# A recurrence and a gated layer in one kernel: three units of 512 tokens in the ramp, y in two tiles, and a new order list

## The chip, the cores and the metric

The kernel runs on one core of one Trainium2 chip. The metric is the device time of one execution in microseconds (us), median of three. The engines of the core are TensorE (PE, with its weight loads shown as PEld), VectorE (DVE), ScalarE (ACT), GpSimd (POOL) and SyncE (SP), whose queue issues nearly all DMAs. Each takes its instructions in its own order and waits for the others by semaphores.

## The reference

Two stages over 4 sequences of 6,336 tokens, 25,344 tokens of 256 features:

```python
sig = 1.0 / (1.0 + np.exp(-f_logit))
f = lower_bound + (1.0 - lower_bound) * sig
i = 1.0 - f
for t in range(S):
    h = f[:, t] * h + i[:, t] * x[:, t]
    y[:, t] = h
...
H = np.maximum(y @ w_h, 0.0)
T = 1.0 / (1.0 + np.exp(-(y @ w_t + b_t)))
out = T * H + (1.0 - T) * y
```

Input and output are float32. x and f_logit are read once and the output is written once, 25.95 MB each.

## The kernel before

The tokens are cut into 28 units, one after the other: 256, 256, 512, 23 of 1,024, 512 and 256 tokens (`parts`, L42, counts blocks of 128). A unit is loaded with tokens on the partitions, turned so that the 256 features lie in two halves on the partitions, scanned along the tokens, sent through the two matrix products and turned back. Nothing in the kernel picks the order: `order` (L48 to L98) is a list of tokens written out in full, and the loop at its end (L384 to L394) calls `do_<letter>` for each and pins each instruction in its engine's program order. A token such as `b2.1v:0` is step, unit, part or half, `v` for "on VectorE", and the buffer slot after the colon. [...]

The steps of a unit, with engine and line:

- `l`, `x`: loads of f_logit and x, issued by SyncE (L244)
- `u`: sigmoid(-f_logit), which is one minus the sigmoid, on ScalarE (L256)
- `b`: the product bv = u * x, on GpSimd, or on VectorE with `v` (L264)
- `i`: turns u to uT on TensorE, through PSUM (L271); `f`: f = 1 + ncc * uT on ScalarE or, with `v`, VectorE (L280, L282)
- `p`: turns bv to bT on TensorE (L291)
- `s`: the scan y = f * y + bT of one half on VectorE (L308), which reads f from SBUF and bT from PSUM; at the start of a sequence it is cut in two pieces
- `g`, `z`: the two matrix products, of both halves of y, on TensorE (L320, further columns with the same weights L114)
- `t`: the sigmoid of z on ScalarE (L333); `d`: max(g, ncc * y) on VectorE (L337), with y from SBUF and g from PSUM
- `e`: the product d * t, both from SBUF, on GpSimd or, with `v`, VectorE (L343), in the pieces that the fourth entry of a unit gives: 2,048 columns are a whole unit of 1,024 tokens
- `o`: turns y (times a diagonal of cc) and d back and adds them on TensorE (L365, L366); `c`: copies the sum from PSUM on ScalarE or, with `v`, VectorE; `w`: the store, issued by SyncE (L382)

Once only: `pc`, `cc`, `dg` make constants of lower_bound, `pb` and `cb` of the bias, `wt` and `wh` load the weights, `WT` and `WH` scale them on VectorE. The scan's result is kept without the factor 1 - lower_bound = cc, which is put into the weights and the diagonal.

What sets the order around the change:

- Each engine runs its own steps in list order, and waits for the data and for the slot of its result. uT and bT take turns in two PSUM slots (a0, a1), all other PSUM results in three pairs of banks (b0 to b2), at the end the a slots too.
- SyncE's queue holds loads and stores in list order; a store waits there for its copy, and what stands behind it waits too.
- `shared` (L178) remembers the last product of VectorE in the list. The next GpSimd product in the list waits for it. A VectorE product never waits for a GpSimd one that stands ahead of it.

y is one tile of 2,048 columns for each unit, in four slots, the halves side by side (`flat`, `half`).

Of the kernel before, what the change touches and what calls it, by code (L numbers as in the profile page):

```python
# [53 lines left out]
e1.1 e1.0 k*2:0 w0.0 u4:1 z2.0:1 f3.0:1 z2.1:0 b4.0:1 s3.1:0 p3.0:0 o1.0:2 t2.1:0 u27:0 b4.1 c1.0:1 s3.0 w1.0 x8:3  # L54
i4.0:1 g2.0:0 f4.0:0 d2.0 i4.1:1 p4.0:0 l9:1 x9:4 l11:4 t2.0 u5:2 e2.1v e2.0v z3.0:0 g3.1:1 b27.0:0 z3.1:2 s4.0:1
p4.1:0 f4.1:1 i5.0:1 t3.0:0 t3.1 d3.1:1 b5.0:2 g3.0:0 f5.0:0 s4.1 o2.0:1 u6:1 b5.1 c2.0:2 d3.0 w2.0 i5.1:1 x11:0 e3.2
g4.1:2 p5.0:0 d4.1:0 b6.0:1 f5.1:1 s5.0:2 z4.1:0 t4.1:1 p5.1:1 b6.1 u7:2 e3.1 s5.1 l10:0 z4.0:1 t4.0 g4.0:0 i6.0:0
e3.0v p6.0:1 d4.0 o3.0:1 e4.2 b7.0:2 f6.0:0 s6.0:3 e4.0v i6.1:0 b7.1 u8:3 f6.1:1 o3.1:0 c3.0:0 c3.1:1 w3.1 w3.0 g5.0:2
p6.1:0 i8.1:1 z5.0:1 f8.1:0 x10:1 e4.1 t5.0:0 g5.1:0 i7.1:1 b8.0:1 s6.1 i7.0:0 d5.0:1 z5.1:1 l12:2 f7.1:1 p7.1:1 d5.1
f7.0:2 t5.1 b8.1 g6.0:2 p7.0:0 e5.1 k*3:0 o4.1:1 s7.1:0 z6.0:0 d6.0:2 s7.0 u9:1 b9.0:2 g6.1:2 c4.1:3 d6.1 i9.0:1  # L60
t6.0:1 b9.1 o4.0:1 u11:2 i9.1:0 f9.0v:1 c4.0:2 w4.0 e6.0v f9.1:2 g7.1:0 z6.1:2 k*3:1 e5.2v i8.0:1 z7.0:1 e5.0v t6.1
w4.1 f8.0:3 p8.1:0 d7.1:0 t7.0:0 g7.0:2 e6.1 p8.0:1 b11.0:3 o5.0:0 u10:1 c5.0:0 w5.0 x12:2 o5.1:1 c5.1:1 w5.1 s8.1:1
i11.1:0 z7.1:0 f11.1:0 s8.0 b11.1 l13:0 d7.0 p9.0:1 i10.1:0 z8.0:1 e6.2 b10.1:1 g8.1:2 t7.1 f10.1:3 p9.1:0 s9.0:2
# [5 lines left out]
z11.0:2 i13.0:1 p12.0:0 s12.0 o9.0:0 t11.0 f13.0:2 g11.0:1 d11.0 o9.1:2 e11.0 p13.0:1 c9.0:1 u17:1 i14.0:0 f14.0v:1
c9.1:3 g12.0:0 u15:3 d12.0:2 b15.1:2 w9.0 z12.1:1 i17.0:0 f17.0:3 t12.1:1 o10.0:2 s13.0:2 o10.1:0 p13.1:0 c10.0:0  # L70
s13.1 b15.0 c10.1:1 i14.1:1 g12.1:1 z12.0:2 g13.0:0 i15.0:0 l16:1 f14.1:2 d12.1 p14.0:1 x16:2 d13.0:0 t12.0 o11.0:1
w9.1 g13.1:2 s14.0:3 f15.0:0 p14.1:0 o11.1:0 e12.0 w10.0 w10.1 i15.1:1 c11.0:2 u16:2 x17:1 b16.1:1 b16.0 z13.0:1 d13.1
f15.1:1 c11.1:0 z13.1:2 s14.1 t13.1:0 l18:0 t13.0 w11.0 p15.0:1 o12.1:0 i16.0:0 g14.1:2 s15.0:0 d14.1:1 e13.0 o12.0:1
p15.1:1 s15.1 c12.1:1 b17.1:2 f16.0:2 z14.1:0 z14.0:2 p16.0:0 s16.0:1 c12.0:3 t14.1:1 t14.0 g14.0:1 d14.0 i16.1:1
w11.1 l19:1 u18:3 x18:0 b17.0 e14.0 g15.1:0 d15.1:2 z15.0:2 i17.1:0 x19:3 f16.1:0 b18.0:3 p16.1:1 f17.1:1 b18.1 l20:2
s16.1 o13.1:1 t15.0:0 p17.0:0 g15.0:0 w12.1 d15.0 c13.1:0 u19:1 b19.1:1 o13.0:2 p17.1:1 z15.1:1 c13.0:2 z16.0:0
s17.1:2 t15.1 t16.0:1 z16.1:2 s17.0 g16.0:1 w13.1 t16.1 i18.0:1 d16.0:0 g16.1:0 o14.0:2 i18.1:0 f18.0:0 d16.1 e15.0v
# [223 lines left out]
    def half(n, key, h):  # L301
        return st[n][key][:, h * tokens(n):(h + 1) * tokens(n)]

    def do_s(n, h, eng, slot):
        flat(n, "y", "y", slot)
        y = half(n, "y", h)
        for fresh, c, e in pieces(n):
            pin(nc.vector.tensor_tensor_scan(y[:, c:e], st[n]["f", h][:, c:e], st[n]["bT", h][:, c:e],  # L308
# [114 lines left out]
```

## Time and profile before

| | before |
|---|---|
| median of three executions | 207.93 us (207.89 to 208.76) |
| span of the profiled execution, first to last instruction | 206.1 us |
| busy: PE, DVE, ACT, POOL | 192.6, 194.5, 191.9, 173.8 us |
| bytes moved by DMA | 78.7 MB, 382 GB/s over the span |

One execution was profiled; its span is 206.1 us, and no other time of that execution is given. A row of a list by time gives the start and the length in us, engine, line, operation, output and inputs with their shapes, how many like it follow, and in brackets how long the engine sat idle before it and what ended that. A row of a group gives the shape, the count, the busy time, the mean length of one in ns, and the idle time before. A row of a stretch gives the busy time of PE, PEld, DVE, ACT and POOL in it, the granted TensorE clock, the share of the DMA engines and GB/s.

### The profile page before, as it was taken

What the parts mean: (1) busy time and instruction counts of PE and PEld (TensorE: products, weight loads), DVE (VectorE), ACT (ScalarE), POOL (GpSimd) and SP (SyncE); (2) the same over time, 40 slices, a digit from 0 to 9 for tenths busy, and PEclk for the clock granted to TensorE, in tenths of its full rate; (3) what the DMA queues carried; (4) which work ended last, traced back from release to release, by engine and by line L of the source; (5) the groups of instructions that cost most, each with busy time, mean ns of one, the idle gap of its engine ahead of it and who ended that gap; (6) DMA issues with size and microseconds to landing.
All of it is one profiled execution on the core that took longest, in us unless ns stands there. A gap on an engine that the chain in (4) does not pass through costs nothing.

```text
span 206.1 us, 4635 instructions
## 1 busy us (share of the span) xinstructions
PE 192.6 (93%) x1837; PEld 133.8 (65%) x1837; DVE 194.5 (94%) x159; ACT 191.9 (93%) x192; POOL 173.8 (84%) x93
## 2 busy tenths in 40 slices
...
DVE  0899999999999999999899999999999999999972
...
POOL 3036989789979997999999999799899999998840
...
GB/s 196 370 424 422 411 418 423 409 423 417 414 423 408 429 417 426 423 420 413 425 424 416 433 411 417 429 415 418 407 422 422 414 392 378 286 104 204 138 382 248
DMA packets 16125, 78.68 MB, mean 382 GB/s; under 512 B 1764, under 2 KB 2536, under 8 KB 10216
## 3 DMA queue, kind: packets, MB, share of 16 engines
...
q10 hardware_dynamic: 8, 0.00, 0.0%
HBM read 52.43 MB, written 25.95 MB: 380 GB/s over the span
## 4 chain that ended last, share of the span: by engine, by line
PE 53%; ACT 14%; DMA 13%; DVE 10%; issue 6%; POOL 2%; SPq 1%; ACTq 0%; DVEq 0%; POOLq 0%
DMA x<-in_x_dram 9%; DVE y L308 8%; PE op L366 7%; PE bT L291 7%; PE op L365 7%; PE g L320 7%; PE z L320 6%; PE uT L271 6%; PE g L114 6%; PE z L114 6%; ACT o L378 4%; ACT f L282 4%; DMA out_dram<-o 4%; ACT t L333 3%; POOL bv L264 2%
## 5 line engine op out<-in xcount | busy, mean ns | idle before, releaser
L264 POOL TENSOR_TENSOR bv<-u,x 128x1024 bf16<-128x1024 f16 (+1 forms) x49 | 100.9, 2085 | 16.9 <-DVE bt L207 10.7
L308 DVE TENSOR_TENSOR_SCAN y<-f,y,bT 128x1024 bf16<-128x1024 f16 (+5 forms) x54 | 106.8, 1989 | 0.2 <-PE bT L291 0.2
L343 POOL TENSOR_TENSOR d<-d,t 128x512 bf16<-128x512 bf16 (+3 forms) x33 | 73.3, 2234 | 9.6 <-DVE d L343 4.2
L337 DVE SCALAR_TENSOR_TENSOR d<-y,ncc,g 128x1024 bf16<-128x1024 bf16 (+2 forms) x56 | 63.1, 1137 | 1.5 <-PE g L320 1.0
L333 ACT ACTIVATE t<-z,bt 128x1024 bf16<-128x1024 f32 (+2 forms) x56 | 58.9, 1088 | 1.3 <-PE z L114 0.7
L282 ACT ACTIVATE f<-uT,ncc 128x1024 f16<-128x1024 f16 (+2 forms) x51 | 55.4, 1098 | 3.4 <-PE uT L271 2.2
L378 ACT COPY o<-op 128x1024 f32<-128x1024 f32 (+2 forms) x55 | 52.1, 984 | 2.4 <-PE op L366 1.6
L256 ACT ACTIVATE u<-l 128x2048 f16<-128x2048 f32 (+2 forms) x28 | 49.8, 1781 | 2.8 <-DMA l<-in_f_logit_dram 2.7
L366 PE MATMUL op<-ident_b,d 128*128 128x128 bf16 x396 | 49.5, 219 | 0.6 <-DVE d L343 0.6
L365 PE MATMUL op<-diag,y 128*128 128x128 f16 x396 | 49.7, 219 | 0.1
L366 PEld LDWEIGHTS <-d 128*128 128x128 bf16 x396 | 44.0, 113 | 3.2 <-DVE d L343 0.7
L365 PEld LDWEIGHTS <-y 128*128 128x128 bf16 x396 | 44.2, 113 | 1.7
L320 PE MATMUL g<-y,w_sb 128*128 128x512 bf16 (+1 forms) x112 | 39.5, 367 | 0.9 <-DVE d L337 0.7
L320 PE MATMUL z<-y,w_sb 128*128 128x512 bf16 (+1 forms) x112 | 39.3, 367 | 0.4 <-ACT o L378 0.4
L291 PE MATMUL bT<-ident_f,bv 128*128 128x128 f32 x198 | 31.8, 277 | 4.3 <-DVE y L308 2.6
L114 PE MATMUL z<-y,w_sb 128*128 128x512 bf16 x92 | 34.9, 379 | 0.0
L114 PE MATMUL g<-y,w_sb 128*128 128x512 bf16 x92 | 34.9, 379 | 0.0
L320 PEld LDWEIGHTS <-w_sb 128*128 128x128 f16 x224 | 21.6, 98 | 17.5 <-issue 0.9
L271 PEld LDWEIGHTS <-u 128*128 128x128 f16 x396 | 26.3, 98 | 10.2 <-issue 2.6
L271 PE MATMUL uT<-ident_h,u 128*128 128x128 f16 x396 | 31.2, 220 | 1.6 <-DVE y L308 0.8
L291 PEld LDWEIGHTS bT<-ident_f,bv 128*128 128x128 f32 x198 | 22.4, 141 | 12.3 <-ACT f L282 3.0
L114 PEld LDWEIGHTS <-w_sb 128*128 128x128 f16 x184 | 18.0, 98 | 16.7 <-issue 1.8
...
## 6 DMA issues: line engine op xcount, KB each, us to landing
...
l<-in_f_logit_dram SPq DMA_DIRECT2D x23, 1024.0 KB, 12.0
...
```

Of the source, the lines that this page charges most:

```text
L114: return pe.add_instruction(mybir.InstMatmult(name=nc.get_next_instruction_name(), start_tensor_calc=start, stop_tensor_calc=stop, tile_si ...
L264: shared(pin(e.tensor_mul(st[n]["bv"][:, a:c].rearrange("p k d j -> p k j d"), st[n]["u"][:, 2 * a:2 * c].rearrange("p (k j) d -> p k j d" ...
L271: pin(nc.tensor.transpose(uT[:, j * P:(j + 1) * P], st[n]["u"][:, j, h * P:(h + 1) * P], ident_h))
L282: pin(nc.scalar.activation(to, of, AF.Identity, scale=ncc[:, h:h + 1], bias=1.0))
L291: pin(nc.tensor.transpose(words[:, k:k + g * (P - 1) + 1:g], pair, ident_f))
L308: pin(nc.vector.tensor_tensor_scan(y[:, c:e], st[n]["f", h][:, c:e], st[n]["bT", h][:, c:e], 0.0 if fresh else carry[h], op0=ALU.mult, op1 ...
L320: pin(nc.tensor.matmul(p[:, a:e], w, half(n, "y", ki)[:, a:e], start=ki == 0, stop=ki == NH - 1))
L333: pin(nc.scalar.activation(half(n, "t", m), st[n]["z", m][:, :tokens(n)], AF.Sigmoid, bias=bt[:, m:m + 1]))
L337: pin(nc.vector.scalar_tensor_tensor(half(n, "d", m), half(n, "y", m), ncc[:, m:m + 1], st[n]["g", m][:, :tokens(n)], op0=ALU.mult, op1=AL ...
L343: shared(pin(e.tensor_mul(st[n]["d"][:, a:c], st[n]["d"][:, a:c], st[n]["t"][:, a:c])), not eng)
L365: pin(nc.tensor.matmul(o, half(n, "y", h)[:, cols], diag[:, h], start=True, stop=False))
L366: pin(nc.tensor.matmul(o, half(n, "d", h)[:, cols], ident_b, start=False, stop=True))
```

## The change

There are 29 units instead of 28: the one of 512 tokens in the ramp becomes three, and 22 units of 1,024 follow instead of 23. Units 7 to 23 (before: 7 to 21) have their `e` in one piece. y becomes two tiles for each unit, one for each half, in eight slots of 1,024 columns. Store sizes at the end follow the new unit numbers. The list is a new one throughout: `cc` and `dg` stand ahead of the first `b`, the last unit's loads stand late instead of in the ramp, both `b` of unit 2 and one of unit 4 are on VectorE, its `e` past the ramp are `e7.0v`, `e8.0v`, `e16.0v`, `e19.0v`, `e22.0v`, `e26.2v` and `e28.1v` instead of twelve, and one copy of 1,024 columns (`c20.0v`) is on VectorE. The list is cut here to its ends and to lines that the text speaks of.

```diff
--- before.py
+++ after.py
@@ -39,62 +39,63 @@
     firsts = [b * S for b in range(B)]
 
 
-    parts = [2] * 2 + [4] + [8] * 23 + [4] + [2]
+    parts = [2] * 2 + [4] * 3 + [8] * 22 + [4] + [2]
+    bcuts = {2: (0, 1), 4: (0, 1, 2), 8: (0, 2, 4)}
+    ecuts = {2: (0, 256, 512), 4: (0, 512, 1024), 8: (0, 1024, 1536, 2048)}
     units, at = [], 0
     for n, nb in enumerate(parts):
-        units.append((nb, at, {2: (0, 1), 4: (0, 1, 2), 8: (0, 2, 4)}[nb], (0, 2048) if 7 <= n <= 21 else {2: (0, 256, 512), 4: (0, 512, 1024), 8: (0, 1024, 1536, 2048)}[nb]))
+        units.append((nb, at, bcuts[nb], (0, 2048) if 7 <= n <= 23 else ecuts[nb]))
         at += nb * P
     assert at == B * S
     order = """
-l1:0 l0:1 x0:0 x1:1 k*3:a0 l2:2 wt wh x2:2 l3:3 x3:3 l4:4 pc:0 x4:4 u0:0 l27:1 l5:5 b0.0v:0 x27:0 x5:5 u1:1 cc l6:0
-k*3:1 i0.1:0 f0.1:0 dg i1.0:1 b1.0v:1 f1.0:1 k*3:1 k*3:a0 p0.1:1 s0.1:0 i0.0:0 u2:0 f0.0v:0 p0.0:1 s0.0 x6:1 l7:2
-k*3:a0 WT pb:0 k*3:a1 i2.0:0 p1.0:1 f2.0:0 WH k*3:1 s1.0:1 i2.1:0 b2.1v:0 g0.0:1 b2.0 i1.1:1 z0.1:2 f2.1:1 cb f1.1v:2
-z0.0:0 g0.1:a0 p1.1:1 t0.0:0 d0.0:0 k*3:1 d0.1 p2.0:0 s1.1 k*3:0 e0.0v z1.1:1 p2.1:1 t0.1 u3:0 l8:3 g1.1:0 x7:2 s2.0:2
-e0.1 d1.1:1 b3.0:0 z1.0:2 t1.0:0 i3.1:0 f3.1:0 o0.0:0 g1.0:2 c0.0:0 s2.1 d1.0 b3.1v g2.1:2 i3.0:0 d2.1:0 p3.1*3:1 t1.1
...
-e8.0 t10.1:2 e9.0v b13.0:1 z10.0:0 f12.1:2 p11.1:1 b13.1 t10.0 o8.1:1 d10.1:0 p12.1:0 c8.1:0 o8.0:2 s11.1 u14:2
...
-s17.1:2 t15.1 t16.0:1 z16.1:2 s17.0 g16.0:1 w13.1 t16.1 i18.0:1 d16.0:0 g16.1:0 o14.0:2 i18.1:0 f18.0:0 d16.1 e15.0v
...
-d24.0 e23.0v w21.0 c22.1:1 t24.1 w21.1 e24.0 w22.0 i26.0:1 e24.1 z25.0:1 i27.0:0 f26.0:2 g25.0:2 e24.2 i26.1:1 d25.0:0
...
-p27.1:0 e25.1 e25.2v z26.0:2 o25.0:0 o25.1:1 z26.1:a1 s27.1 g26.1:a0 t26.0:0 z27.0:2 c25.0:3 t26.1 c25.1v o25.2:0
-t27.0:1 o25.3:1 d26.1 g27.0:a0 w23.1 z27.1:a1 w24.1 w24.0 e26.0 c25.2:0 e26.1v o26.0:2 o26.1:0 d27.0:0 g27.1:a0 d27.1
-w25.0 c25.3 t27.1 e27.0 e27.1v o27.0:1 c27.0v:1 c26.0:2 o27.1:a0 c26.1 w25.1 w26.0 w27.0 c27.1:3 w27.1
+l1:0 l0:1 u1:0 u0:1 pc:0 k*2:1 i0.1:0 cc x0:0 dg x1:1 pb:1 b0.0v:0 i1.0:1 f1.0:0 k*3:0 i1.1:1 f0.1:1 b1.0v:1 f1.1:2 i0.0:0
+l3:2 wh f0.0:3 wt l2:3 u3:2 k*1:0 p0.0:1 x2:2 p0.1:0 s0.0:0 x3:3 s0.1:1 k*2:0 p1.0:1 k*1:0 p1.1:0 s1.0:2 l4:4 k*5:0 i3.0:1
+s1.1:3 WH cb f3.0:3 i3.1:0 k*1:0 g1.0:2 WT g0.0:0 d1.0:0 d0.0:1 f3.1:1 g0.1:1 z1.1:2 u2:3 d0.1 b2.0v:2 b2.1v g1.1:0 i2.1:1
+z0.0:1 i2.0:0 f2.1:0 p2.1:1 t0.0:0 f2.0:2 z0.1:1 d1.1 z1.0:0 p2.0:0 t1.1:1 b3.1:3 b3.0 t1.0 s2.1:4 u4:1 l5:5 s2.0:5 t0.1
+p3.1:1 e1.1v i4.1:0 z2.0:2 x4:4 f4.1:0 e0.0v x5:5 e1.0v e0.1v u5:0 k*2:0 p3.0:0 o1.0:0 g2.0:1 s3.1:6 s3.0:7 b4.0v:0 d2.0:2
+i4.0:1 i5.1:0 b4.1 f4.0v:2 c1.0:0 t2.0:2 g2.1:0 l6:0 z3.0:2 f5.1:1 z2.1:1 p4.1:1 d2.1 t3.0:1 x6:0 i5.0:0 g3.1:2 s4.1:2 t2.1
+z3.1:0 f5.0:3 b5.1:1 b5.0 p4.0:1 d3.1:0 e2.1 t3.1 u6:3 b6.1:2 b6.0 e2.0 o0.0:1 g3.0:2 s4.0:3 k*3:0 z4.0:0 p5.0:0 t4.0:0
...
+f12.1:1 d8.0:0 d8.1 b12.0:3 b11.0:0 b11.1 z9.1:1 f10.0:3 c6.0:0 i11.0:1 o6.1:2 p10.0:0 t9.1:2 b12.1 z9.0:0 c6.1:2 f11.0:2
+e7.0v w6.1 g9.0:1 t9.0 x13:1 e8.0v s10.0:6 o7.1:2 d9.0:2 u13:0 i11.1:1 p10.1:0 g9.1:0 s10.1:7 f11.1:3 o7.0:1 c7.0:1 p11.0:1
...
+w14.1 z17.0:2 g17.0:1 s18.1:6 b20.1:3 t17.1:1 l22:4 b20.0 u21:3 i20.0:1 p18.0:0 t17.0 w12.1 e16.0v d17.0:0 s18.0:7 f20.0:3
...
+c18.1:0 i23.0:0 f23.0:2 u28:1 x24:0 z21.0:0 g20.0:2 p22.1:0 e19.0v s22.0:6 l25:2 d20.0 g21.1:1 t21.0:2 o19.0:0 i23.1:1
...
+z22.0:2 i28.1:1 f28.1:0 s23.1:4 g22.1:1 i24.0:1 w18.1 t22.0:0 w18.0 d22.1:1 o20.1:0 p23.0:0 e21.0 x25:1 g22.0:2 z22.1:1
...
+p24.1:0 f25.0:2 t23.1:1 z23.0:2 t23.0 w19.1 w20.0 u26:2 b26.0:2 e22.0v s24.1:2 b26.1 p24.0:1 g23.0:0 o22.0:1 g23.1:2 i25.1:0
...
+d24.1 e23.0 o23.1:1 e24.0 u27:3 i28.0:1 f28.0:2 w22.1 w21.1 c23.1:3 o23.0:0 c23.0:0 e24.2 e24.1 p26.1:1 z25.1:2 s26.0:6
+b27.1:0 b27.0 t25.1:0 z25.0:1 g25.0:0 t25.0 s26.1:7 o24.0:2 i27.1:0 g25.1:1 c24.0:2 p27.1:1 d25.0:1 f27.1:1 d25.1 o24.1:2
+i27.0:0 g26.0:0 z26.0:1 b28.0:3 e25.0 s27.1:4 p27.0:1 f27.0:3 c24.1:1 e25.1 t26.0:1 d26.0:0 e25.2 z26.1:2 p28.1:0 e26.0
+g26.1:0 t26.1 s27.0:5 z27.0:a1 o25.2:1 o25.3:2 s28.1:2 w24.0 w24.1 w23.1 t27.0:2 p28.0:0 g27.0:a1 d26.1 w23.0 c25.3:2 e26.1
+o25.0:0 c25.2 s28.0:3 o25.1:2 d27.0:2 e26.2v g27.1:a0 d27.1 w25.1 c25.0:1 z27.1:a1 o26.1:1 c25.1 o26.0:0 t27.1 e27.0 o26.3:2
+c26.1v:3 c26.0 e27.1 g28.0:a0 w25.0 o26.2:1 z28.0:a1 c26.3:0 c26.2 d28.0:1 o27.0:0 o27.1:2 t28.0:0 w26.0 c27.1:2 c27.0v e28.0
+g28.1:a0 w26.1 z28.1:a1 t28.1 d28.1 e28.1v o28.0:1 w27.0 o28.1:a0 c28.1v:1 c28.0:3 w28.0 w28.1
 """
 
     NU = len(units)
@@ -299,10 +300,12 @@
         return st[n][key]
 
     def half(n, key, h):
+        if key == "y":
+            return st[n][key, h][:, :tokens(n)]
         return st[n][key][:, h * tokens(n):(h + 1) * tokens(n)]
 
     def do_s(n, h, eng, slot):
-        flat(n, "y", "y", slot)
+        st[n]["y", h] = sb([P, NB * P], BF16, "y", slot)
         y = half(n, "y", h)
         for fresh, c, e in pieces(n):
             pin(nc.vector.tensor_tensor_scan(y[:, c:e], st[n]["f", h][:, c:e], st[n]["bT", h][:, c:e],
@@ -343,13 +346,13 @@
         shared(pin(e.tensor_mul(st[n]["d"][:, a:c], st[n]["d"][:, a:c], st[n]["t"][:, a:c])), not eng)
 
     def store(n):
-        return 1 if n in (27,) else 4
+        return 1 if n == 28 else 4
 
     def blocks(n, q):
         return q * store(n), min((q + 1) * store(n), units[n][0])
 
     def part(n, k):
-        w = min(2 if n in (24, 25, 26,) else 4, store(n))
+        w = min(2 if n in (25, 26, 27) else 4, store(n))
         return k * w, min(k * w + w, units[n][0])
 
     def do_o(n, k, eng, slot):
```

66 lines of the change are left out of this document (28 added, 38 removed).

## The prediction

> **What bounds the kernel now.** I read the page's busy shares and its 40 slices first, then busy time by stretch, then the instructions of VectorE (DVE) and GpSimd (POOL) in order of time, and last the groups by shape.
>
> ```profile
> span 206.1 us, 4635 instructions
> ...
> PE 192.6 (93%) x1837; PEld 133.8 (65%) x1837; DVE 194.5 (94%) x159; ACT 191.9 (93%) x192; POOL 173.8 (84%) x93
> ...
> DVE  0899999999999999999899999999999999999972
> ...
> POOL 3036989789979997999999999799899999998840
> ...
> GB/s 196 370 424 422 411 418 423 409 423 417 414 423 408 429 417 426 423 420 413 425 424 416 433 411 417 429 415 418 407 422 422 414 392 378 286 104 204 138 382 248
> ```
>
> ```profile
> 0.00:5.00 5.00, 3.81 (x10) 1.31 (x11) 0.27 (x1) 2.42 (x4) 1.62 (x11) 1.00 0.62 192
> 5.00:10.00 5.00, 3.96 (x20) 1.75 (x18) 4.16 (x12) 2.16 (x4) 0.00 (x0) 1.00 1.03 364
> ...
> 195.00:200.00 5.00, 5.00 (x69) 4.25 (x67) 4.37 (x8) 4.89 (x11) 2.33 (x2) 1.00 0.90 356
> 200.00:206.00 6.00, 1.63 (x22) 1.05 (x19) 1.29 (x4) 1.71 (x4) 0.67 (x1) 0.83 0.71 272
> ```
>
> Behind the length, the stretches list TensorE, its weight loads, VectorE, ScalarE (ACT) and GpSimd. VectorE is full between its two ends: 194.5 us of work in 206.1, and most of the 11.6 idle ones lie before 5.52 us and after 195. So the end is set by when VectorE starts, by what its list holds, by what it waits in the middle, and by what follows its last scan. ScalarE is nearly as full (93%), but no wait of VectorE's between 10 and 195 stands beside it; GpSimd has 32 us to spare. DMA moves 0.42 MB per us from 10 us on.
>
> **The change, part by part.**
>
> *The start.* Ramp rows of VectorE, ScalarE and GpSimd:
>
> ```profile
> 5.52 0.73 DVE L264 TENSOR_TENSOR bv<-u,x 128x512 bf16<-128x512 f16 x1 [4.39 <-DMA x<-in_x_dram]
> 6.15 0.14 DVE L200 TENSOR_SCALAR ncc<-lbT 128x2 f32<-128x2 f32 x1
> ...
> 7.19 0.72 DVE L264 TENSOR_TENSOR bv<-u,x 128x512 bf16<-128x512 f16 x1
> 7.87 0.69 DVE L308 TENSOR_TENSOR_SCAN y<-f,bT 128x256 bf16<-128x256 f16 x1
> ```
>
> ```profile
> 4.12 1.15 ACT L256 ACTIVATE u<-l 128x512 f16<-128x512 f32 x2 [1.27 <-DMA l<-in_f_logit_dram]
> ```
>
> ```profile
> 12.91 1.17 POOL L264 TENSOR_TENSOR bv<-u,x 128x512 bf16<-128x512 f16 x1 [10.67 <-DVE bt L207]
> 15.00 0.68 POOL L343 TENSOR_TENSOR d<-d,t 128x256 bf16<-128x256 bf16 x1 [0.92 <-DVE d L343]
> 16.40 2.14 POOL L264 TENSOR_TENSOR bv<-u,x 128x1024 bf16<-128x1024 f16 x1 [0.72 <-DMA x<-in_x_dram]
> ```
>
> `cc` and `dg` now run behind `b0.0v`, from 6.15 to 7.19: 1.04 us. The new list puts them ahead of it, into VectorE's wait for x0, whose four first loads keep their places in SyncE's queue. That is a gain of 1.0 us. Against it, four `f` of 256 tokens now stand on ScalarE between the two `u` (ending at 5.27) and the first scan. At 0.42 each (the 0.476 of VectorE's own `f` below, less overlap) and 0.25 for the first transposes (an estimate) the fourth ends near 7.2, where VectorE, after two `b`, would be free at 6.9; bounds 0 and 0.6, I take 0.4 lost. Later ramp waits: `b2.0v` needs x2. In the old queue x3, landing at 16.40, ended the first 4.72 MB; the new x2 ends the first 3.15 MB, so at 0.42 MB per us it lands 3.7 earlier, at 12.7, and VectorE's list reaches it at 12.6. No loss to speak of, and no margin.
>
> *VectorE's work.* The rows by shape:
>
> ```profile
> L264 POOL TENSOR_TENSOR bv<-u,x 128x1024 bf16<-128x1024 f16 x45 | 96.2, 2165 | 5.4 <-DVE d L343 3.0 <-PE bT L291 1.3 <-DMA x<-in_x_dram 0.9
> L308 DVE TENSOR_TENSOR_SCAN y<-f,y,bT 128x1024 bf16<-128x1024 f16 x40 | 92.8, 2334 | 0.2 <-PE bT L291 0.2
> L337 DVE SCALAR_TENSOR_TENSOR d<-y,ncc,g 128x1024 bf16<-128x1024 bf16 x46 | 57.4, 1258 | 0.4 <-issue 0.3
> ...
> L343 POOL TENSOR_TENSOR d<-d,t 128x2048 bf16<-128x2048 bf16 x12 | 49.1, 4096 | 0.1
> ...
> L343 POOL TENSOR_TENSOR d<-d,t 128x512 bf16<-128x512 bf16 x15 | 17.4, 1172 | 4.8 <-DVE d L343 2.6 <-ACT t L333 1.1 <-ACT f L282 1.1
> ...
> L308 DVE TENSOR_TENSOR_SCAN y<-f,y,bT 128x512 bf16<-128x512 f16 x4 | 5.1, 1270 | 0.0
> ...
> L343 DVE TENSOR_TENSOR d<-d,t 128x1024 bf16<-128x1024 bf16 x6 | 4.5, 756 | 0.0
> ...
> L343 DVE TENSOR_TENSOR d<-d,t 128x2048 bf16<-128x2048 bf16 x3 | 3.9, 1295 | 0.0
> L280 DVE TENSOR_SCALAR f<-uT,ncc 128x1024 f16<-128x1024 f16 x3 | 3.8, 1274 | 0.0
> ...
> L337 DVE SCALAR_TENSOR_TENSOR d<-y,ncc,g 128x512 bf16<-128x512 bf16 x4 | 2.9, 729 | 0.2 <-PE g L320 0.2
> ...
> L264 DVE TENSOR_TENSOR bv<-u,x 128x512 bf16<-128x512 f16 x3 | 2.2, 721 | 4.4 <-DMA x<-in_x_dram 4.4
> ...
> L343 DVE TENSOR_TENSOR d<-d,t 128x512 bf16<-128x512 bf16 x5 | 2.0, 420 | 0.1
> ...
> L264 DVE TENSOR_TENSOR bv<-u,x 128x1024 bf16<-128x1024 f16 x1 | 1.8, 1753 | 0.0
> ...
> L280 DVE TENSOR_SCALAR f<-uT,ncc 128x256 f16<-128x256 f16 x2 | 1.0, 476 | 0.1
> ...
> L376 DVE COPY o<-op 128x512 f32<-128x512 f32 x1 | 0.7, 692 | 0.2 <-PE op L366 0.2
> ...
> L343 DVE TENSOR_TENSOR d<-d,t 128x256 bf16<-128x256 bf16 x2 | 0.6, 278 | 0.1
> ```
>
> Counted in the two lists: scans, four of 512 for two of 1,024: +0.41. `d`, the same: +0.40. `b` on VectorE, two of 512 more and the one of 1,024 gone: -0.31. `e` on VectorE, six of 1,024 and two of 512 gone, two of 2,048 and three of 256 more: -1.95. `f`, two of 256 gone, one of 512 more (between 0.476 and 1.274, 0.75 taken): -0.20. `c`, one of 512 more and one of 1,024 (0.69 to 1.38, 1.22 taken): +1.91. Sum +0.26, less 0.2 for three more overlaps of 0.07: nothing. GpSimd takes `e` over: three more of 1,024 (as a `b`, 2.165), two more `b` of 512 (1.17), one `b` of 1,024 and three `e` of 256 (0.68) fewer: +4.6 us, hidden only while it keeps ahead of the scans. ScalarE has two copies fewer and more of the small pieces, TensorE seven idle matmuls fewer and the same columns otherwise: nothing on VectorE's path, and -0.5 to 0.5 if one of them were the bound. y in two tiles lets a half go when its own readers are done, but `o` reads both halves last, so I cost it at nothing, between -0.3 and 0.3.
>
> *Products of VectorE beside those of GpSimd.* Two pairs of rows show what happens when they meet:
>
> ```profile
> 123.70 6.40 POOL L264 TENSOR_TENSOR bv<-u,x 128x1024 bf16<-128x1024 f16 x3
> ```
>
> ```profile
> 129.76 1.42 DVE L343 TENSOR_TENSOR d<-d,t 128x2048 bf16<-128x2048 bf16 x1
> ```
>
> ```profile
> 186.65 2.30 POOL L343 TENSOR_TENSOR d<-d,t 128x512 bf16<-128x512 bf16 x2
> ```
>
> ```profile
> 188.48 1.02 DVE L343 TENSOR_TENSOR d<-d,t 128x1024 bf16<-128x1024 bf16 x1
> ```
>
> GpSimd ends at 130.10 and 188.95; VectorE's product ends 1.1 and 0.55 after that, whenever it began. So it stands still until GpSimd's product is over, and a collision costs VectorE from nothing to a whole 4.1 us. The wait that `shared` adds works one way only: a GpSimd product listed behind one of VectorE's waits, and one listed ahead doesn't. In the new list many are listed ahead (five before `e16.0v`, four before `e22.0v`, `b12.0 b11.0 b11.1 b12.1` before `e7.0v`), so there it is the two engines' progress that decides. I add each engine's rows in list order, less overlaps. GpSimd's first three products wait for x3 and for `b4.0v` (20.0 to 20.7), the fourth starts at 20.7:
>
> - `e3.1v`: VectorE 25.7 (5.52, 19.8 of work, 0.4), GpSimd free at 26.0: 0.3 lost; `e3.0v` then behind `e2.1`: 0.45.
> - `e7.0v`: VectorE 62.45 (55.8 of work: ten scans of 1,024, six of 512, four of 256 and what lies between), GpSimd at the end of `b12.0` 63.0 (from 20.7: 14 `b`, ten `e`, 41.65, and 0.65 of its own waits): 0.55.
> - `e16.0v`: 125.1 against 125.2, the end of `e15.0`: 0.15. `e19.0v`: 150.55 against 151.35: 0.8. `e22.0v`: 168.6 against 169.0: 0.4.
>
> Together 2.65, with 0.4 of the ramp 3.05.
>
> [...]
>
> *The end.*
>
> ```profile
> 194.75 0.73 DVE L308 TENSOR_TENSOR_SCAN y<-f,y,bT 128x256 bf16<-128x256 f16 x1
> ...
> 202.07 0.43 DVE L376 COPY o<-op 128x256 f32<-128x256 f32 x1 [0.32 <-PE op L366]
> ```
>
> ```profile
> 200.24 0.67 POOL L343 TENSOR_TENSOR d<-d,t 128x256 bf16<-128x256 bf16 x1 [1.79 <-DVE d L337]
> ```
>
> Up to the last unit's first scan the old list holds 187.5 us of VectorE work: 5.52 + 187.5 = 193.0 against 194.75 traced, so 1.75 was lost to waits. The new one holds 185.8: 5.52 + 185.8 + 3.05 = 194.4. Behind that scan the old list has 5.4 us of work, 2.35 of waits and 3.6 for the last store, 11.35 to the end. The new one has 6.8 of work (a `d` of 512 more there and a 512 copy), 0.4 for `e26.2v` behind `e26.0`, 0.8 to 1.9 of waits, and the same store: 12.1. The span comes out at 206.5. GpSimd checks it: from `e25.0` at 190.3 its last nine products take 10.4 and some 0.6 of waits, end near 201.3; the old last one ended at 200.9 and the span 5.2 later, which gives 206.5 too. So +0.4 on the span of 206.1; the span is 1.8 below the median 207.93 of the three runs, and I add the difference to the median: 208.3.
>
> **The rivals.** *The products do keep apart.* The sums of two engines over 160 us are good to a microsecond at best, and four of the five meetings came out within 0.8 of a GpSimd boundary, which speaks for a list laid to meet them. Then only the ramp's 0.4 and 0.6 of collisions remain: 192.3 + 11.6 = 203.9 of span, 205.7. Against it: at `e3.0v` and `e7.0v` GpSimd's products are listed ahead and back to back, with nothing that makes room.
>
> *The lock goes to the other at each release.* At `e7.0v e8.0v`, `b11.0` has stood ready since 63.0 when `e7.0v` ends; if it gets in between, `e8.0v` waits a whole `b`, 2.1 us: 210.4. It decides as soon as `b12.0` ends after `e7.0v` has begun. For it: GpSimd is full there. Against it: VectorE's instructions follow each other with an overlap of 0.07, leaving no gap. [...]
>
> *GpSimd becomes the bound.* From 20.7 it has 173.8 us of products; with the 6.5 us of waits counted above it ends at 201. The old trace shows 15.8 of waits (200.9 less 12.9, less the 172.2 busy after the first 5 us). Each microsecond over 6.5 arrives at the end, and `b27.0` is then late for `s27.1`: at 15.8 it is 217.6, at 9.5, which I take, 211.3. For it: 176.0 us of products in all, less overlaps, against 171.4 before. Against it: half the old waits come before VectorE's products, of which there are fewer now.
>
> **How the numbers follow.** VectorE as the bound with a few collisions 0.34, at 208.3 (206.8 to 209.4); kept apart 0.32, at 205.7; the lock going over 0.20, at 210.4; GpSimd as the bound 0.14, at 211.3. What can be told from no change is 0.5%, 206.9 to 209.0. Faster than that: the second case nearly whole and the first's lower edge, 0.34. The same: 0.27. Slower: 0.39. The range reaches from 204.8 (the second case with none of the collisions) to 212.0.
>
> **What would show it.** Right: `cc` and `dg` before 5 us, the first scan between 6.9 and 7.4; `e7.0v`, `e19.0v` and `e22.0v` longer than 1.2 us by what GpSimd's running product has left; GpSimd's first large gap up to `b4.1` and no other over 2.5; the last unit's first scan near 194.4. Wrong: any scan that waits for `bT` with GpSimd behind it, or VectorE idle in the ramp after 7.4 (x2 late), or TensorE holding a `d` or scan back for a PSUM slot in the middle.

## The result and the profile after

The changed kernel took 225.75 us (median of four runs, 224.41 to 226.1) beside 207.91 for the kernel before on the same chip: a ratio of 1.082, 95% interval 1.075 to 1.088. It is 8% slower. The forecast was 208.3 us with a range to 212.0; the profiled span is 223.8 us where 206.5 was worked out, 17.3 more. Some executions run at a lower granted clock (the share of TensorE's full speed that the chip allows) and take longer (one of the kernel before 250.5 us at 0.754, another 207.83 at 0.997); times and ratios below are of the others, unless the text gives the clock.

The page of the changed kernel: span, busy times, the slices of VectorE and of the granted clock, and the transfer rate.

```profile
span 223.8 us, 4587 instructions
...
PE 197.9 (88%) x1803; PEld 135.9 (61%) x1830; DVE 205.4 (92%) x162; ACT 192.3 (86%) x196; POOL 180.3 (81%) x94
...
DVE  2799999999999979999998998999999999799972
...
PEclk9999999999998579999999999999999999999997
...
GB/s 209 392 416 427 417 417 417 413 426 417 420 144 286 275 117 332 327 344 425 426 414 416 373 398 337 424 417 417 398 320 423 389 287 349 274 280 234 283 342 241
```

VectorE is busy 10.9 us longer, though its list holds the same work to about a microsecond. The clock and the transfers, flat in the middle before, break down: the clock from about 67 to 83 us, the transfers from 62 to about 100. VectorE's rows by time show the ramp first:

```profile
2.88 0.16 DVE L201 TENSOR_SCALAR ncc<-lbT 128x2 f32<-128x2 f32 x1 [1.75 <-PE lbT L195]
...
5.86 1.34 DVE L265 TENSOR_TENSOR bv<-u,x 128x512 bf16<-128x512 f16 x2 [1.83 <-DMA x<-in_x_dram]
8.47 0.69 DVE L311 TENSOR_TENSOR_SCAN y<-f,bT 128x256 bf16<-128x256 f16 x1 [1.27 <-PE bT L292]
...
62.32 1.27 DVE L340 SCALAR_TENSOR_TENSOR d<-y,ncc,g 128x1024 bf16<-128x1024 bf16 x1
63.51 8.75 DVE L346 TENSOR_TENSOR d<-d,t 128x2048 bf16<-128x2048 bf16 x1
```

`cc` and `dg` moved into the wait for x0 as said, but the first scan comes at 8.47, not near 7.2. The last row is `e7.0v`: 8.75 us for a product that takes 1.2 alone (1.21 for `e8.0v` right behind it). GpSimd's rows beside it, the four in one row and the last of them by itself:

```profile
62.74 8.44 POOL L265 TENSOR_TENSOR bv<-u,x 128x1024 bf16<-128x1024 f16 x4
```

```profile
69.05 2.14 POOL L265 TENSOR_TENSOR bv<-u,x 128x1024 bf16<-128x1024 f16 x1
```

These are `b12.0 b11.0 b11.1 b12.1`, back to back at their usual 2.15 us. `b12.0` was running when `e7.0v` began; three more began after it and went first, while VectorE's product stood still (the stand, from here on). VectorE's product ended 1.07 us behind the last of them, when GpSimd's list had come to `b13.0`, which waits for `e8.0v` through `shared`. So at the end of a product of GpSimd's the engine that stands need not be next: here it was not, three times over. What the two meet at the expectations call the port; the rows show that one of two products stands, not what makes it stand.

Behind the stand, TensorE's and ScalarE's first rows, each with the wait before it in brackets:

```profile
72.32 0.30 PE L369 MATMUL op<-ident_b,d 128*128 128x128 bf16 x1 [5.12 <-DVE d L346]
```

```profile
75.75 1.11 ACT L283 ACTIVATE f<-uT,ncc 128x1024 f16<-128x1024 f16 x1 [5.66 <-DVE y L311]
```

And the stretches around it, of the kernel after and then of the kernel before: busy time of PE, PEld, DVE, ACT, POOL, then granted clock, share of the DMA engines and GB/s.

```profile
60.00:66.00 6.00, 5.82 (x70) 4.51 (x70) 6.00 (x4) 6.00 (x7) 6.00 (x4) 1.00 0.59 244
66.00:72.30 6.30, 1.20 (x7) 0.41 (x5) 6.30 (x2) 4.09 (x4) 5.18 (x3) 0.89 0.83 231
72.30:77.00 4.70, 3.94 (x28) 3.38 (x29) 4.66 (x4) 1.11 (x1) 2.14 (x1) 0.50 0.86 361
77.00:83.00 6.00, 5.78 (x50) 4.71 (x50) 5.20 (x3) 2.73 (x3) 2.48 (x1) 0.66 0.15 59
```

```profile
60.00:66.00 6.00, 5.35 (x60) 3.75 (x58) 6.00 (x5) 6.00 (x7) 6.00 (x4) 1.00 1.00 406
66.00:72.30 6.30, 6.30 (x69) 4.88 (x68) 6.30 (x5) 6.30 (x7) 6.30 (x3) 1.00 1.03 425
72.30:77.00 4.70, 4.70 (x52) 3.49 (x51) 4.66 (x3) 4.70 (x6) 4.70 (x4) 1.00 1.00 417
77.00:83.00 6.00, 6.00 (x57) 4.14 (x55) 6.00 (x5) 6.00 (x6) 4.68 (x2) 1.00 1.02 423
```

TensorE did nothing for 5.12 us, and its granted clock was then 0.50 for 4.7 us and 0.66 in the six behind them. In the kernel without the stand (the first experiment) the clock was 1.00 in each of these stretches. After how long without work it falls, no run shows. The transfers, at 406 to 425 GB/s in these stretches before, fall to 59. SyncE's queue says why:

```profile
67.99 0.45 SPq L245 DMA_DIRECT2D l<-in_f_logit_dram  x1
81.31 0.33 SPq L385 DMA_DIRECT2D out_dram<-o  x1
81.69 0.43 SPq L245 DMA_DIRECT2D l<-in_f_logit_dram  x1
```

The store `w7.0` waits 13 us for ScalarE's copy of unit 7, which the stand has made late, and `l15` waits behind it. The first dip, 244 GB/s at 60 to 66, is earlier than the stand: there SyncE stands at `w6.1`, which it issues at 66.30, 12 us behind its last load.

So two theories for the 17.3 us. A: it is the stand at `e7.0v`, directly and through what it delays. B: the stand is a part, and the rest lies in the list itself.

### The profile page after: what moved, and what is told of

Its sections match the earlier page's. It is cut to its first block, busy times and chain, and to the rows that moved or that the text cites. A ratio compares the mean times of both kernels' runs of the same rounds, so it can differ in the third digit from the quotient of the medians.

```text
span 223.8 us, 4587 instructions
## 1 busy us (share of the span) xinstructions
PE 197.9 (88%) x1803; PEld 135.9 (61%) x1830; DVE 205.4 (92%) x162; ACT 192.3 (86%) x196; POOL 180.3 (81%) x94
## 4 chain that ended last, share of the span: by engine, by line
PE 47%; DVE 16%; DMA 14%; ACT 9%; issue 9%; POOL 3%; SPq 1%; DVEq 0%; ACTq 0%; POOLq 0%
DVE y L311 10%; PE g L323 7%; PE bT L292 7%; PE z L323 6%; PE op L369 6%; PE op L368 6%; PE uT L272 6%; DMA l<-in_f_logit_dram 5%; DMA x<-in_x_dram 5%; ACT o L381 4%; PE g L115 4%; DMA out_dram<-o 4%; PE z L115 4%; DVE d L340 3%; DVE d L346 2%
## 5 line engine op out<-in xcount | busy, mean ns | idle before, releaser
L265 POOL TENSOR_TENSOR bv<-u,x 128x1024 bf16<-128x1024 f16 (+1 forms) x50 | 102.8, 2081 | 28.5 <-DVE bv L265 13.1
L346 POOL TENSOR_TENSOR d<-d,t 128x512 bf16<-128x512 bf16 (+3 forms) x33 | 77.4, 2364 | 8.9 <-DVE d L340 7.5
L283 ACT ACTIVATE f<-uT,ncc 128x1024 f16<-128x1024 f16 (+2 forms) x54 | 54.1, 1015 | 13.0 <-PE uT L272 6.7
L369 PE MATMUL op<-ident_b,d 128*128 128x128 bf16 x396 | 51.1, 223 | 6.4 <-DVE d L346 6.0
L381 ACT COPY o<-op 128x1024 f32<-128x1024 f32 (+2 forms) x53 | 48.9, 940 | 8.9 <-PE op L369 5.1
L368 PE MATMUL op<-diag,y 128*128 128x128 f16 x396 | 51.4, 222 | 2.5 <-ACT o L381 2.1
L292 PE MATMUL bT<-ident_f,bv 128*128 128x128 f32 x198 | 33.5, 286 | 3.8 <-POOL bv L265 1.2
L272 PE MATMUL uT<-ident_h,u 128*128 128x128 f16 x396 | 32.1, 223 | 2.3 <-ACT u L257 1.1
L323 PEld LDWEIGHTS <-w_sb 128*128 128x128 f16 x232 | 22.3, 98 | 17.3 <-issue 0.9
L115 PE MATMUL g<-y,w_sb 128*128 128x512 bf16 x79 | 30.2, 382 | 0.0
L115 PEld LDWEIGHTS <-w_sb 128*128 128x128 f16 x176 | 17.3, 98 | 20.2 <-issue 6.6
L115 PE MATMUL z<-y,w_sb 128*128 128x512 bf16 x76 | 28.8, 379 | 0.1
## 6 DMA issues: line engine op xcount, KB each, us to landing
x<-in_x_dram SPq DMA_DIRECT2D x22, 1024.0 KB, 12.1
```

Of the source, the lines that this page charges most:

```text
L115: return pe.add_instruction(mybir.InstMatmult(name=nc.get_next_instruction_name(), start_tensor_calc=start, stop_tensor_calc=stop, tile_si ...
L265: shared(pin(e.tensor_mul(st[n]["bv"][:, a:c].rearrange("p k d j -> p k j d"), st[n]["u"][:, 2 * a:2 * c].rearrange("p (k j) d -> p k j d" ...
L272: pin(nc.tensor.transpose(uT[:, j * P:(j + 1) * P], st[n]["u"][:, j, h * P:(h + 1) * P], ident_h))
L292: pin(nc.tensor.transpose(words[:, k:k + g * (P - 1) + 1:g], pair, ident_f))
L323: pin(nc.tensor.matmul(p[:, a:e], w, half(n, "y", ki)[:, a:e], start=ki == 0, stop=ki == NH - 1))
L346: shared(pin(e.tensor_mul(st[n]["d"][:, a:c], st[n]["d"][:, a:c], st[n]["t"][:, a:c])), not eng)
```

## The experiments

Times are medians; each ratio is to the kernel before on the same chip. The runs come from several chips, on which the kernel before took 207.9 to 208.9 us, so between two edits a ratio tells more than a difference of times. In diffs of the list only the tokens that move and their neighbours stand; `...` marks what is left out.

**The stand taken away.** Three of the four products go behind `e8.0v`.

```diff
 b12.0:3
-b11.0:0 b11.1
...
-b12.1
...
 e7.0v
...
-e8.0v
+e8.0v b11.0:0 b11.1 b12.1
```

> The changed kernel with three GpSimd products (b11.0, b11.1, b12.1) listed behind e8.0v, so that they wait for it; nothing else differs. Theory A (VectorE's product stands still for as long as GpSimd has a next product ready, and most of what is lost later follows from that one stand): e7.0v takes at most 2.6 us instead of 8.75, and the time falls from 225.8 to 207 to 212. Rival B (the stand costs its own 7.5 us, and the later 7.6 come from the new order by itself): 216 to 219. Rival C (e7.0v stood for something else than GpSimd's products): e7.0v stays near 8.7 us, 225 to 226.

218.75 us, ratio 1.048 (1.045 to 1.051): 7 us less than the changed kernel. (219.35, which later expectations name, is the median of all six executions.) The row of `e7.0v`:

```profile
63.29 2.55 DVE L346 TENSOR_TENSOR d<-d,t 128x2048 bf16<-128x2048 bf16 x1
```

What is left of its collision is the rest of `b12.0`. That the stand costs some 7 us is shown, and so is that some 10 us over the kernel before are not the stand: B.

**y in two tiles alone**, in the kernel before.

```diff
     def half(n, key, h):
+        if key == "y":
+            return st[n][key, h][:, :tokens(n)]
...
-        flat(n, "y", "y", slot)
+        own = st[n].setdefault("ys", slot)
+        st[n]["y", h] = sb([P, NB * P], BF16, f"y{h}_", own)
```

> The kernel before with y in two tiles for each unit and nothing else. Theories A and B: the same time within 0.5 us, 207.4 to 208.4. Rival D (two tiles bring waits of their own): slower by more than 1 us.

208.56 us, ratio 1.000 (0.998 to 1.002). Within the noise it costs nothing.

**The kernel before without the wait that `shared` adds.**

```diff
-        if not gpsimd:
+        if True:
             held[:] = [ins]
```

> The kernel before without the waits of GpSimd's products for VectorE's (no data depends on them). Theory A: where GpSimd's next product is ready, VectorE's product stands for more than one GpSimd product; at least one of the 2,048 and 1,024 column products takes over 3 us, and the time grows by 2 to 10 us. Rival B' (the port changes hands at each GpSimd product's end): no product over 2.2 us beyond its own length except beside a product of 2,048 columns, time 207.5 to 209.5.

222.2 us, ratio 1.067 (1.062 to 1.072), more than the 2 to 10 us expected. The profiled execution took 237.47 us at a mean granted clock of 0.956, so only the order of its rows is used. VectorE's longest product, and GpSimd's rows beside it:

```profile
137.85 11.52 DVE L343 TENSOR_TENSOR d<-d,t 128x2048 bf16<-128x2048 bf16 x1
```

```profile
135.84 4.27 POOL L264 TENSOR_TENSOR bv<-u,x 128x1024 bf16<-128x1024 f16 x2
140.06 4.05 POOL L343 TENSOR_TENSOR d<-d,t 128x2048 bf16<-128x2048 bf16 x1
144.07 4.22 POOL L264 TENSOR_TENSOR bv<-u,x 128x1024 bf16<-128x1024 f16 x2
```

VectorE's product stands in the old list too, past four products that began after it, once nothing holds GpSimd back. That wait is worth 7%, and it explains the rows on which the prediction priced a collision. These are GpSimd's rows right behind them, in the kernel before:

```profile
131.26 2.15 POOL L264 TENSOR_TENSOR bv<-u,x 128x1024 bf16<-128x1024 f16 x1 [1.16 <-DVE d L343]
...
189.64 2.14 POOL L343 TENSOR_TENSOR d<-d,t 128x1024 bf16<-128x1024 bf16 x1 [0.69 <-DVE d L343]
```

Both times GpSimd's next product was waiting for VectorE's. "VectorE ends soon after GpSimd's product" and "soon after GpSimd runs dry" were the same thing there.

**The meeting by itself**: a small kernel in which VectorE's product meets a row of GpSimd's, in 11 kinds, twice each; and again with ScalarE, TensorE and the transfers at work, in 18 rounds.

> The output is not computed; only meetings of the two engines' products are, in eleven kinds, each twice: GpSimd has three to six products ready one behind the other, VectorE's product comes 0.2 to 1.6 us into the first. Theory A: VectorE's product ends only after GpSimd's last in every kind (4 b: 8.4 us and more). Rival B': it ends one product of its own after the GpSimd product that ran when it came. Rival E (it depends on the kind: same form behind same form keeps the port, or a request ahead of the next product's dispatch gets it): A for some kinds and B' for others, the same in both repeats.

> Its output is not computed. 18 rounds of four products of GpSimd of 1,024 tokens each, against one product of VectorE of 2,048 columns that arrives 0.1 to 2 us after the first of them has started, with ScalarE, TensorE and the transfers at work on other tiles; the same without that work changed hands at the end of the running product in all its rounds. Theory L (what else runs decides who gets the port): in at least 3 of 18 rounds VectorE's product stands past two or more products of GpSimd. Rival M: none stands past more than one, and what decides it stays open.

In all 22 meetings and in 17 of the 18 (in the other round VectorE came first) VectorE's product stood behind one product of GpSimd at most. In the 18 rounds VectorE's products took 2.02 us on average, and GpSimd's 72 took 2.37 where 2.15 is usual. One of the loaded rounds, VectorE's row and that of GpSimd's next product:

```profile
160.88 3.10 DVE L65 TENSOR_TENSOR d<-d,t 128x2048 bf16<-128x2048 bf16 x1
```

```profile
162.85 3.14 POOL L59 TENSOR_TENSOR bv<-u,x 128x1024 bf16<-128x1024 f16 x1
```

GpSimd's next product is recorded from 162.85 but takes 3.14 us, one more than usual: it stood while VectorE's ran. Four kinds of queue, arrivals over 2 us and the load of the others made no difference. In the kind in which VectorE has two products one behind the other, a product of GpSimd's went between them both times, and the second took 3.04 us: the order of the prediction's second rival. What lets GpSimd go first several times is not found. In the full kernels it isn't fixed by the place either: `e16.0v` behind `b19.1` took 3.05 us in the changed kernel (one product stood for), and 9.26 in a kernel below (four).

**Loads ahead of stores.** The next theory for the 10 us was SyncE's queue: each load from the tenth unit on goes ahead of up to two stores, first without the stand, then in the changed kernel itself.

```diff
-w6.1 x13:1 w5.1 l14:2 w7.0 l15:3
+l14:2 w6.1 l15:3 w5.1 x14:2 w7.0
```

> The changed kernel with the three products of GpSimd behind `e8.0v` (219.35 us), and on SP's queue each load from the tenth unit on moved ahead of up to two stores that stood before it; nothing else moves. Theory D: what is left of the loss is that a store waiting for ACT's copy holds the loads behind it on SP's queue, and the transfers, which were busy 93.6% of the span before (192.9 of 206.1 us), can't make up the time. Then the stretches with 8 to 229 GB/s near 66 and 89 us fill, the waits of VectorE for bT (2.49 us at 94.6, 1.42 at 184.3) and its two waits for d and g near 99 and 188 go, and the time falls by 4 to 7 us, to 212 to 215 us. Rival E: VectorE is late by its list alone and the loads wait for it, not the other way round; the time stays within 1% of 219.35 (217 to 221.5 us), and the waits come back at other places.

> The changed kernel itself (225.75 us) with only that edit of SP's queue. GpSimd's four products still stand ahead of `e7.0v`, so its 8.75 us stay by both theories (8 to 10 us between its start and its end). Theory D: the stores that wait behind the stand no longer hold the loads, transfers go on through it, and the time falls by 4 to 8 us, to 218 to 222 us. Rival E: 223.5 to 227.5 us.

229.73 us and 231.15 us, ratios 1.102 (1.095 to 1.108) and 1.110 (1.107 to 1.114): slower by 11 and 6 us by the ratios. Both theories were wrong.

In the second kernel the stand, which the expectation had kept, did not come. VectorE's two products, `e7.0v` and `e8.0v`, and GpSimd's between them:

```profile
70.61 1.22 DVE L337 TENSOR_TENSOR d<-d,t 128x2048 bf16<-128x2048 bf16 x1
71.74 3.17 DVE L337 TENSOR_TENSOR d<-d,t 128x2048 bf16<-128x2048 bf16 x1
```

```profile
70.69 3.15 POOL L256 TENSOR_TENSOR bv<-u,x 128x1024 bf16<-128x1024 f16 x1
```

Here the two engines took turns, again as the prediction's second rival had it. So the new order of loads cost this kernel more than the 6 us, as the stand's 7 were no longer in it.

ScalarE's row at the first large gap of the first of the two kernels:

```profile
60.07 1.01 ACT L372 COPY o<-op 128x1024 f32<-128x1024 f32 x1 [4.75 <-DMA out_dram<-o]
```

The stores now come so late that ScalarE has no buffer for its copies (11.1 us of such waits in all, 3.0 before the edit). Putting the loads ahead as a whole costs more than it gains.

**`cc` and `dg` first, alone**, in the kernel before.

```diff
-b0.0v:0 x27:0 x5:5 u1:1 cc l6:0
+cc dg b0.0v:0 x27:0 x5:5 u1:1 l6:0
```

> The kernel before with `cc` and `dg` issued ahead of `b0.0v` on VectorE, as the changed kernel does, and nothing else moved: the part of the change that the prediction put at 1.0 us gained. If the ramp is bound by VectorE's first operations, the first scan starts 0.9 to 1.1 us earlier and the time falls to 206.5 to 207.5 us. Rival: the ramp is bound by the first transfers and the products behind them (the changed kernel's first scan started at 8.47 us, not at 7.2 as forecast), the gain is eaten within the ramp, and the time is 207.6 to 208.6 us.

208.34 us, ratio 1.001 (1.000 to 1.003). The first scan came at 7.09 instead of 7.87, and the gain was lost again in one group of VectorE's:

```profile
L343 DVE TENSOR_TENSOR d<-d,t 128x512 bf16<-128x512 bf16 x5 | 3.5, 711 | 0.1
```

Before, these five took 2.0 us, 420 ns each. One of them, at 24.68, now met a `b` and took 1.90 us. That row lost 1.5 us: being early by 0.8 us moved a product into a collision.

**Fewer bytes.** From the tenth unit on, units of 1,024 tokens load only half of their x and use it twice, which leaves out part of the computation: without the stand, in the changed kernel, and in the kernel before.

```diff
-        pin(nc.sync.dma_start(t[:, :nb], rows(src, n, 0, nb)))
+        half = name == "x" and n >= 9 and nb == NB
+        r = rows(src, n, 0, nb)
+        if half:
+            nb //= 2
+        pin(nc.sync.dma_start(t[:, :nb], r[:, :nb]))
...
+        xo = 0 if n >= 9 and units[n][0] == NB else 2 * a
...
-                                st[n]["x"][:, 2 * a:2 * c].rearrange("p (k j) d -> p k j d", j=2))), not eng)
+                                st[n]["x"][:, xo:xo + 2 * (c - a)].rearrange("p (k j) d -> p k j d", j=2))), not eng)
```

> The changed kernel with the three products of GpSimd behind `e8.0v` (219.35 us); from the tenth unit on, each unit of 1,024 tokens loads only the first half of its x and uses it for both of its products, so that some 8.4 of the 78.4 MB are not moved (16 units of 0.5 MB) and all instructions of the engines stay. Theory F: what is left of the loss is that transfers are a second bound beside VectorE (busy 192.9 of 206.1 us before), so that what they lose while SP stands behind a store can't be made up; with 20 us fewer of them it can, VectorE's waits for bT at 94.6 and 184.3 go, and the time falls by 4 to 8 us, to 211 to 215 us. Rival G: the waits come from the order of the products alone (ACT, TensorE and GpSimd in each other's way); the time stays at 217 to 221 us.

> The changed kernel itself (225.75 us) with the same half of x left out. GpSimd's four products still stand ahead of `e7.0v`: 8 to 10 us between its start and its end. Theory F: of the 17.8 us lost the stand's 7.5 stay and most of the rest goes: 215 to 220 us. Rival G: 223 to 227 us.

> The control: the kernel before with the same half of x left out. Both theories: VectorE bounds it and no transfer is late, so it stays within 1% of 207.9 us (206 to 209 us). A fall below 206 us would say that transfers bound the kernel before as well.

The page counts 9.4 MB fewer in the changed kernel and 8.9 in the kernel before, where 8.4 was expected. The changed kernel: 222.46 us, 1.065 (1.060 to 1.070), 3.3 less and between the two ranges. The kernel before: 207.92, 0.997 (0.994 to 1.001): transfers don't bound it. The kernel without the stand fell in two groups, three runs at 222.1 to 222.6 and one at 214.08, so no ratio is given. In its profiled run, one of the three, `e16.0v` and GpSimd's four products:

```profile
127.55 9.26 DVE L351 TENSOR_TENSOR d<-d,t 128x2048 bf16<-128x2048 bf16 x1
```

```profile
127.27 8.46 POOL L270 TENSOR_TENSOR bv<-u,x 128x1024 bf16<-128x1024 f16 x4
```

A second stand, of four products; that the run at 214.08 was without it fits its time but isn't shown, since it has no trace.

**The other stands taken away**, with all of x and with half.

```diff
-b20.1:3
...
-b20.0
...
-e16.0v
+e16.0v b20.1:3 b20.0
...
-b25.1:1 b25.0
...
-b26.0:2 e22.0v
+e22.0v b25.1:1 b25.0 b26.0:2
```

> The changed kernel with GpSimd's products that could run against `e7.0v`, `e16.0v` and `e22.0v` all moved behind them: the three behind `e8.0v` as before (219.35 us), and now `b20.1 b20.0` behind `e16.0v` and `b25.1 b25.0 b26.0` behind `e22.0v`. All theories of the port: `e16.0v` takes 1.2 us where it took 2.98 to 9.26 for the same place, `e22.0v` at most 1.7, and no run of it stands long, so the runs lie close together. Theory F (transfers lost while SP stands behind a store can't be made up): VectorE's waits for bT near 94 and 184 us stay, 215 to 219 us. Rival G (the loss after the stands comes from the order of the products): also 215 to 219 us; the next kernel parts them.

> The same, with the second half of x left out from the tenth unit on (the first half is used twice). Of the four runs of the kernel without the two new moves three had `e16.0v` in a long stand (9.26 us in the profiled one) and took 222.2 us; the fourth took 214.08. Theory F: with the stand gone all runs lie at 211 to 214 us, 3 us or more below the kernel with all of x, and VectorE has no wait over 1 us between 20 and 200 us. Rival G: within 1% of the kernel with all of x.

218.72 us, 1.047 (1.041 to 1.053), and 214.82 us, 1.034 (1.026 to 1.042). `b19.1 b19.0` also stand ahead of `e16.0v` and were not moved, so it still took 2.79 and 5.09 us.

These two kernels ran on one chip and differ in nothing but the half of x, so they show best what the transfers do. All of x, then half: busy time between 20 and 200 us of PE, PEld, DVE, ACT, POOL, then clock, share of the DMA engines and GB/s.

```profile
20.00:200.00 180.00, 168.81 (x1609) 116.33 (x1606) 173.07 (x115) 169.47 (x159) 164.74 (x73) 0.99 0.95 370
```

```profile
20.00:200.00 180.00, 170.48 (x1637) 118.43 (x1636) 179.01 (x118) 171.74 (x163) 168.34 (x77) 1.00 0.85 324
```

VectorE was idle for 6.9 us there with all of x and for 1.0 with half, in no wait over 0.5 us, as theory F said; the kernel before has 1.2. The ratio fell by 0.013, about 3 us: less than the waits, and less than expected, since `e16.0v` stood 2.3 us longer.

**One store, and one store the other way.** In the changed list `x13 w5.1 l14` go ahead of `w6.1`, the stop that runs the transfers dry near 64 us; in the kernel before `w7.0` goes ahead of `l14 x14`.

```diff
-w6.1 x13:1 w5.1 l14:2
+x13:1 w5.1 l14:2 w6.1
```

```diff
-l14:1 x14:1 w7.0
+w7.0 l14:1 x14:1
```

> The kernel with three products protected and all of x (218.72 us), and `x13`, `w5.1` and `l14` issued ahead of `w6.1` on SP. In the kernel without the last two moves SP stood at `w6.1` from 54.4 to 66.1 us with these behind it, and the transfers ran dry from 62 us on (8 to 74 GB/s). Theory F: they no longer run dry there, x and l come in time near 94 us, VectorE's waits of 2.25 and 1.38 us near 95 and 99 us go or shrink, 215 to 217.5 us. Rival J: those waits come from the later stops of SP (`w7.0`, `w9.0`) alone: 218 to 220 us. A third, that the stores come late for their buffers as in the kernel with all loads moved: above 220 us.

> The kernel before with one edit on SP: `w7.0` ahead of `l14` and `x14` instead of behind them. The store was issued at 71.9 us, the two loads at 63.9 and 64.5. Theory F: SP stands some 8 us with the loads behind it, transfers run dry, and since they were busy 93.6% of the span they don't make it up: 211 to 216 us. Rival K: buffers loaded ahead cover it, 207.7 to 209 us.

217.53 us, 1.046 (1.044 to 1.048): at theory F's weak end, but the ratio is not clear of the 1.047 without this edit. The waits of 2.25 and 1.38 us near 95 and 99 us shrank to 0.25 and nothing, and others, of 0.9 and 1.2 us, came elsewhere; the transfers now sag from 70 us on instead of 60. The kernel before went to 210.16 us, 1.010 (1.006 to 1.015), between the two ranges. Its transfer rate:

```profile
GB/s 193 399 418 421 408 422 419 414 419 413 422 424 418 422 419 378 366 423 421 413 421 411 432 418 413 418 420 420 412 423 416 415 397 396 286 93 203 145 370 249
```

The expectation had taken SyncE's rows two positions too early: in the kernel before the two loads were issued at 72.7 and 73.3 us and the store at 76.8, and in this one the loads at 77.3 and 77.8. So the stop that it made was 4.6 us, not 8. It dents two slices to 378 and 366 GB/s and costs about 2 us, clear of zero but under 2%. The changed list makes longer ones, 12 us at `w6.1` and 13 at `w7.0`.

**All stands gone**, `b12.0` and `b19.1 b19.0` moved too, with half of x and with all.

```diff
-b12.0:3
...
-e8.0v b11.0:0 b11.1 b12.1
+e8.0v b12.0:3 b11.0:0 b11.1 b12.1
...
-b19.1:0
...
-b19.0
...
-e16.0v b20.1:3 b20.0
+e16.0v b19.1:0 b19.0 b20.1:3 b20.0
```

> The kernel with three products protected and half of x left out (216.08 us; in its profiled run of 213.0 us VectorE had no wait over 0.5 us between 20 and 200 us, and `e16.0v` still took 5.09 us past `b19.1 b19.0`, `e7.0v` 2.49 past the rest of `b12.0`). Now `b12.0` as well goes behind `e8.0v`, and `b19.1 b19.0` behind `e16.0v`. Theory F plus the port: what was left was the 3.9 and 1.3 us of these two, so the span falls to 207 to 209 us, 209 to 211 as time, level with the kernel before. Rival H: GpSimd, with seven products held back, becomes late itself and VectorE waits for its products: 213 us or more, as time 214 to 218.

> The computation whole again: the kernel with `x13 w5.1 l14` ahead of `w6.1` (217.53 us), and now `b12.0` behind `e8.0v` and `b19.1 b19.0` behind `e16.0v` as in the kernel with half of x that took 213.14 us. If stands and transfers add up, the stands' 2.9 us (1.3 at `e7.0v`, 1.6 at `e16.0v`) come off: 214 to 216 us, with waits of VectorE for x and l left that the half-x kernel doesn't have. If what is taken from the stands comes back as waits for transfers, since these are the bound of this list: 216.5 to 218 us.

213.14 us (213.04 to 214.0), 1.026 (1.023 to 1.029), and 217.19 us (216.65 to 217.51), 1.037 (1.030 to 1.045; the kernel before took 207.9 to 210.5 us on that chip). The first lies between its two expectations. The pages, half of x and then all of it:

```profile
span 211.3 us, 4588 instructions
...
DVE  2699999999999989999999999999999999899971
```

```profile
span 215.1 us, 4589 instructions
...
DVE  2699999999999989999889998999999999699971
...
GB/s 192 369 420 426 416 413 417 420 417 424 415 427 416 274 356 238 292 430 422 419 420 382 382 378 356 424 421 411 405 401 414 340 334 352 265 296 189 280 340 233
```

With all of x the gain of 2.9 us at the two stands shrank to 0.3 us by the time, within the second expectation, and to some 2 by the ratio (1.046 to 1.037), whose intervals overlap; so times alone don't decide. The profiles speak for the second: VectorE's busy time fell by 2.6 us (198.6 to 196.0) and the span by 0.5. VectorE is held up a little in many slices, and the transfers still sag, to 274, 356, 238 and 292 GB/s from 70 to 91 us. With half of x most of VectorE's delays go. The two kernels differ by 2.4 us by the ratios and by 4 by the times, but in the place of `w6.1` and in the chip too, so this is no second measure of the transfers. Of the edits of the changed list that leave nothing out, the best is 3.7% slower than the kernel before, which stays the fastest.

## Why the prediction was wrong

The 206.5 us of span forecast and the 223.8 measured part at the last unit's first scan: 210.58 against 194.4, 16.2 late. The rest, 1.1, is the tail. Up to that scan the trace has 10.6 us of collisions where 2.65 were forecast, 7.8 us of VectorE's waits where 0.4 were, and 0.5 more work; it began 0.3 later.

- *The start.* Half right. `cc` and `dg` run before 5 us. The first scan came at 8.47, not 6.9 to 7.4, waiting 1.27 us for bT. 1.1 us of this is left at `e7.0v` (63.51 against 62.45). The part tried alone, in the kernel before, gave 0.8 us at the first scan and nothing at the end.
- *VectorE's work, y, GpSimd's work.* Right. Up to the last unit's first scan VectorE's list holds 186.35 us where 185.8 was worked out, two tiles of y cost nothing, and GpSimd, with 180.3 us against 173.8, kept gaps of 2 us and more: it was not the bound.
- *The collisions: the step that failed.* "So it stands still until GpSimd's product is over, and a collision costs VectorE from nothing to a whole 4.1 us", hence 0.55 at `e7.0v`. It was reached 1.1 us late, while `b12.0` ran, as reckoned, and cost 7.5 us. The price here was that of the whole row of products listed ahead without a wait: what is left of `b12.0` and 6.3 for three more. The text named all four tokens and then counted one. VectorE came 1.1 us and GpSimd 1.9 us later than reckoned, so it is in part luck that they met there at all. The others: `e3.1v` 0.6 (0.3 said), `e3.0v` 0.2 (0.45), `e22.0v` 0.45 (0.4), `e19.0v` 0 (0.8), and `e16.0v` 1.8 (0.15). Taking the stand away gave 7 us.
- *What was not costed: the transfers.* The sum has 0.4 us for VectorE's waits in the ramp and nothing for those in the middle, without a reason: the prediction read 0.42 MB per us off the page and went no further. The middle had 6.5 us of them. The transfers were busy 93.6% of the old span, 192.9 us, so a list that stops SyncE in front of loads has little to make it up with. The new one does so at `w6.1` before anything is late, and at `w7.0` for 13 us because of the stand. With half of x VectorE's idle time between 20 and 200 us fell from 6.9 us to 1.0 and the time by some 3 us (1.047 to 1.034); in the kernel before half of x is worth nothing.
- *The rest.* 213.14 against 208.3 leaves 4.8 us: 0.9 in the ramp, 1.1 in the tail (13.2 us behind that scan, 12.1 said), and 2.8 in the middle, with half of x and with 1.7 us of collisions where 2.65 were forecast; VectorE has five waits of 0.3 to 0.7 us there. Which part of the list makes these was not tried, so the cause of this part stays open.
- *The rivals.* "The products do keep apart" fell at four places. "The lock goes to the other at each release" was right for `e16.0v` and `e22.0v`, whose GpSimd successors took 3.14 us, and for the pair `e7.0v e8.0v` in the second kernel with the loads ahead, but not for that pair in the changed kernel: `e8.0v` took 1.21, with GpSimd dry. The case that came, one product of VectorE past several of GpSimd, was in none of them.
